# A gated linear recurrence with a low-rank mixer: the first pair's up product taken early and put right later, a bitwise sign, wider filler matmuls and a new order

## The chip, the cores and the metric

The kernel runs on one core of one Trainium2 chip. The metric is the device time of one execution in microseconds. The kernel before took 640.84 us in the median of three runs (638.37 to 641.07).

## The reference

Two blocks stand one behind the other. The first is a recurrence over 768 tokens for 4 batches and 8 heads of 48 channels, with a complex decay for each channel; the second mixes tokens through a rank of 32 and channels through a hidden layer of 1536.

```python
mag = np.sqrt(a_re * a_re + a_im * a_im)
scale = np.minimum(mag, 0.999) / (mag + 1e-06)
ar, ai = a_re * scale, a_im * scale
for t in range(S):                       # S_re, S_im: 48 x 48 per head
    new_re = ar[t] * S_re - ai[t] * S_im
    new_im = ar[t] * S_im + ai[t] * S_re
    S_re, S_im = new_re + k[t] (x) v[t], new_im
    y[t] = q[t] @ S_re
x = y, heads side by side                # 4 x 768 x 384
u = x + (xT @ U @ V)T                    # U: 768 x 32, V: 32 x 768
out = u + np.maximum(u @ w_ch1, 0) @ w_ch2
```

All values are float32.

## The kernel before, in words

**Tiles.** A chunk is 128 tokens of one batch, so there are 24 chunks, six for each batch; a group is two chunks, and a pair of chunks is also the unit of the second block (`mixer(m)`, m from 0 to 11).

**Gates (`gates(g)`).** For a group, the real and imaginary parts of the gates are loaded (`ar`, `ai`), and ACT and DVE turn them into log magnitudes `l` (tile `GL`; from the fourth group on two rounded halves, `GS`) and angles in turns `z` (kept in `y`). The angle takes the sign of `ar`, kept in `n`: in group 0 DVE makes plus or minus one half (`is_ge` and a subtraction, line 656), in the others ACT takes Sign (line 374 is the helper's). Then `z` is the product of `n` and an arctangent less a quarter of pi (line 737), followed by a scale and the addition of 0.25, on DVE in group 0 (line 740) and on ACT as Identity in the others. TensorE forms running sums over tokens by products with triangular matrices: `es ps` and `ef ps` from `l` (line 674), `tot` for block totals (line 712), `ph` from `z` (line 776). ACT's Exp of these gives the factors `es`, `ef` and `E`; Sin of the phase `F` gives `cs`.

**Chunks (`prep(i)`, `chain(i)`).** `prep` multiplies q and k with the factors (`qk`, `QKC`) and transposes them (`tr`, line 834) into `QK`. `chain` forms the products of queries and keys inside blocks (`inner`, lines 884 and 881; `corners`, line 948), scales `QK` between them on DVE, collects the masked blocks in `DG`, moves them by DMA to `AT`, forms the state (`dk`, line 973; `GM`, `G`) and the output `y` (lines 1004 and 1012), which ACT copies into `xo`.

**Mixer.** Once the six chunks of a batch are there, `rank` (line 1047) sums over them with U, ACT copies the result to `r`. For each pair, `spread` multiplies with V (`mixed`, line 1066), DVE adds to `xo`, TensorE transposes (`uTp`), and `uT` feeds the up product: six calls of `up(ff)`, each of two times three matmuls 128x256 (line 1094), whose result ACT copies through Relu to `h`. `down` (lines 1241 and 1284) multiplies `h` with the second weight, DVE adds to `xo`, and a DMA writes it. Pairs from the eighth on take a form with fewer products (`few`, line 1152).

**Order.** Nothing is scheduled when the program runs. Every operation is recorded in `Plan` with its engine and its kind; the table `ORDER` gives each one a place in one list, and `Plan.order()` sorts by it. Every engine executes its own part of that list in order. A second table, `SPARE`, says how many filler matmuls (`idle`, line 1414: the identity with itself, 128x128, into the PSUM tile `spare`) stand ahead of a place. A unit of `SPARE` is one such matmul; a matmul of float32 shows as two records in the profile. In all there are 147 units, 23 of them ahead of the first `es ps`.

**Weights.** The weights come as 64-bit words, 768 KB a piece, and DVE (for later pieces ACT too) converts them (lines 556 to 562); the first pieces are converted in the same stretch as the first chunks.

Of the kernel before, what the change touches and what calls it, by code (L numbers as in the profile page):

```python
# [10 lines left out]
FP = mybir.dt.float32  # L11
# [4 lines left out]
OP = mybir.AluOpType  # L16
# [10 lines left out]

ORDER = {
    ("SP", "load"): {0.1: [5], 1.2: [19], 1: [18], 2: [20], 3.5: [73, 76], 7: [415, 206, 413, 497, 276, 172, 204, 250, 251], 5.1: [99], 5.6: [154],
        6.1: [252], 6.6: [311], 7.1: [492], 7.6: [562], 8.1: [570], 8.6: [620], 9.1: [641], 9.6: [656], 0.0: [2, 1, 2652, 2641, 2654], 0.05: [4, 3],  # L30
        3: [70, 69, 72, 74], 1.3: [71, 68], 1.4: [67], 2.5: [77, 75], 2.6: [209], 5.7: [113, 156], 6: [210], 6.7: [171, 170], 7.7: [312, 279], 8:
        [282], 8.7: [408, 368], 9: [491, 364, 365, 414, 392], 11: [499, 557, 556, 601, 808], 9.7: [604, 488], 10: [560], 10.7: [603, 569], 13: [655,
        643, 682, 644, 976], 11.7: [683, 684], 12: [914], 12.7: [783, 742], 15: [784, 886, 818, 816, 1043], 13.7: [887, 888], 14: [1040], 14.7: [927,
        928], 17: [975, 1041, 1049, 1025, 1307], 15.7: [1057, 1056], 16: [1155], 16.7: [1159, 1154], 19: [1179, 1180, 1237, 1291, 1493], 17.7: [1308,
        1281], 18: [1391], 18.7: [1330, 1366], 21: [1328, 1369, 1454, 1397, 1675], 19.7: [1496, 1453], 20: [1495], 20.7: [1492, 1491], 23: [1591,
        1563, 1578, 1643, 1866], 21.7: [1676, 1677], 22: [1781], 22.7: [1756, 1754], 25: [1837, 1835, 1780, 1867, 2161], 23.7: [1836, 1838], 24:
        [1941], 24.7: [1947, 1943], 25.7: [2162, 2166], 26: [2173], 26.7: [2177, 2167], 27: [2353]},
    ("POOL", "load"): {0: [13], 1.5: [59], 2: [12], 1: [28]},
    ("DVE", "load"): {1: [40]},
    ("DVE", "w1"): {0: [34, 42, 39, 62, 65], 1: [61, 60, 66, 86, 96], 2: [118, 115, 125, 137, 145], 3: [168, 164, 189, 213, 224], 4: [259, 262, 290],  # L40
        5: [355, 379, 429], 6: [348, 381, 559]},
    ("ACT", "w1"): {4: [219, 200], 5: [302, 359], 6: [329, 373]},
    ("ACT", "w2"): {0: [544, 543], 2: [588, 589], 4: [597, 598], 6: [649, 640], 8: [658, 661], 10: [677, 695]},
    ("DVE", "w2"): {0: [565, 566, 568], 2: [593, 594, 605], 4: [606, 621, 624], 6: [651, 653, 654], 8: [659, 670, 671], 10: [699, 700, 703], 12: [704,
        740, 755]},
    ("ACT", "gates"): {0: [0, 7, 6, 11, 16, 21, 23, 36, 53, 43, 44, 45, 55, 58], 1: [14, 8, 22, 29, 30, 37, 46, 54, 48, 49, 52, 57], 2: [127, 104,
        105, 89, 128, 131, 130, 132, 134, 176, 182, 149, 160, 159, 173, 178, 179, 180, 194, 193, 196], 4: [270, 221, 253, 294, 272, 287, 286, 299,
        301, 330, 351, 315, 326, 325, 327, 337, 336, 342, 360, 356, 361], 6: [438, 393, 417, 418, 448, 454, 453, 455, 457, 466, 472, 480, 504, 505,
        503, 508, 509, 510, 496, 495, 511], 8: [582, 584, 602, 583, 610, 612, 613, 618, 619, 623, 627, 628, 660, 650, 657, 664, 665, 667, 639, 638,
        668], 10: [711, 728, 731, 698, 746, 748, 752, 761, 764, 777, 798, 760, 810, 812, 815, 834, 831, 823, 804, 782, 836], 12: [876, 924, 929, 898,  # L50
        932, 944, 950, 952, 951, 986, 997, 973, 981, 982, 985, 1010, 1008, 1011, 993, 994, 1033], 14: [1117, 1106, 1108, 1152, 1135, 1136, 1137, 1173,
        1138, 1174, 1197, 1178, 1196, 1199, 1195, 1212, 1213, 1220, 1208, 1219, 1221], 16: [1273, 1274, 1299, 1272, 1316, 1318, 1317, 1321, 1320,
        1336, 1337, 1322, 1380, 1365, 1363, 1406, 1408, 1402, 1382, 1379, 1413], 18: [1465, 1508, 1506, 1512, 1517, 1518, 1524, 1526, 1529, 1525,
        1537, 1558, 1555, 1557, 1556, 1569, 1567, 1574, 1573, 1568, 1575], 20: [1669, 1665, 1678, 1698, 1697, 1709, 1725, 1734, 1726, 1720, 1735,
        1826, 1771, 1770, 1766, 1800, 1797, 1801, 1774, 1789, 1802], 22: [1889, 1893, 1907, 1890, 1913, 1915, 1914, 1919, 1918, 1933, 1958, 1956,
        1963, 1960, 1957, 1977, 1967, 1969, 1946, 1962, 1978]},
    ("DVE", "gates"): {0: [10, 9, 17, 25, 27, 63, 24], 1: [15, 26, 33, 35, 38, 64, 41], 2: [117, 144, 151, 186], 4: [261, 313, 314, 352], 6: [427,
        465, 473, 475, 483, 535], 8: [607, 622, 632, 633, 634, 642], 10: [736, 753, 765, 766, 776, 799], 12: [931, 945, 961, 966, 969, 1023], 14:
        [1113, 1153, 1185, 1187, 1189, 1236], 16: [1313, 1319, 1339, 1343, 1344, 1358], 18: [1510, 1519, 1544, 1546, 1547, 1559], 20: [1687, 1719,
        1738, 1747, 1748, 1777], 22: [1908, 1926, 1936, 1937, 1939, 1979]},  # L60
    ("PE", "gates"): {0: [31, 32, 51], 1: [47, 50, 56], 2: [158, 161, 174, 175, 192, 191], 4: [323, 324, 335, 340, 343, 341], 6: [502, 501, 506, 507,
        487, 486], 8: [646, 647, 663, 666, 635, 637], 10: [803, 811, 822, 821, 781, 780], 12: [980, 983, 1007, 1006, 992, 991], 14: [1193, 1192, 1211,
        1217, 1204, 1218], 16: [1364, 1356, 1403, 1401, 1381, 1371], 18: [1550, 1549, 1564, 1571, 1572, 1565], 20: [1769, 1764, 1796, 1799, 1773,
        1783], 22: [1959, 1945, 1966, 1968, 1944, 1955]},
    ("SP", "totals"): {0: [98, 79, 80, 97], 2: [198, 208, 195, 211], 4: [410, 409, 411, 391], 6: [498, 558, 500, 561], 8: [741, 681, 685, 680], 10:
        [817, 805, 990, 890], 12: [1157, 1055, 1170, 1042], 14: [1368, 1276, 1367, 1241], 16: [1393, 1392, 1383, 1396], 18: [1755, 1588, 1593, 1594],
        20: [1832, 1942, 1833, 1798], 22: [2176, 2187, 2175, 2174]},
    ("ACT", "angles"): {0: [78, 87, 92, 93, 100], 1: [84, 101, 107, 111, 110], 2: [197, 202, 220, 236, 232, 238, 239, 246, 248, 249], 4: [363, 376,
        390, 406, 396, 397, 398, 421, 430, 431], 6: [545, 564, 587, 615, 626, 673, 674, 708, 707, 710], 8: [669, 675, 709, 750, 773, 841, 842, 813,
        875, 864], 10: [838, 845, 877, 974, 900, 1036, 1037, 1065, 1074, 1071], 12: [1050, 1067, 1081, 1143, 1216, 1267, 1248, 1269, 1245, 1270], 14:  # L70
        [1238, 1246, 1271, 1327, 1346, 1435, 1415, 1462, 1461, 1464], 16: [1414, 1439, 1480, 1531, 1614, 1616, 1615, 1619, 1617, 1668], 18: [1603,
# [1398 lines left out]
```

## Time and profile before

| | |
|---|---|
| median of three runs | 640.84 us (638.37 to 641.07) |
| profiled execution, its span | 641.9 us |
| TensorE busy | 622.8 us (97%) |
| VectorE busy | 509.9 us (79%) |
| ScalarE busy | 396.8 us (62%) |
| spare matmuls | 294 records, 43.9 us busy, from 1.4 to 125.7 us |
| up product of the first pair | from 126.6 us |
| granted clock of TensorE | 0.992 in the mean |

The page gives no time outside the span, so the profiled execution is taken at 641.9 us, 1.1 above the median. "Busy" is the union of an engine's instructions. Matmuls overlap in the array, so a busy TensorE is not one at its full rate, and a record is longer than the distance to the next: where many stand back to back, the distance is what one costs. The window rows show, for each stretch, its length and then, for each engine, the busy time and the count; behind them the clock that TensorE was granted, the busy share of the DMA engines and GB/s. A line in order of time has its start, its length, the engine and line, and in brackets the idle time before it with what ended it.

### The profile page before, as it was taken

What the parts mean: (1) busy time and instruction counts of PE and PEld (TensorE: products, weight loads), DVE (VectorE), ACT (ScalarE), POOL (GpSimd) and SP (SyncE); (2) the same over time, 40 slices, a digit from 0 to 9 for tenths busy, and PEclk for the clock granted to TensorE, in tenths of its full rate; (3) what the DMA queues carried; (4) which work ended last, traced back from release to release, by engine and by line L of the source; (5) the groups of instructions that cost most, each with busy time, mean ns of one, the idle gap of its engine ahead of it and who ended that gap; (6) DMA issues with size and microseconds to landing.
All of it is one profiled execution on the core that took longest, in us unless ns stands there. A gap on an engine that the chain in (4) does not pass through costs nothing.

```text
span 641.9 us, 23713 instructions
## 1 busy us (share of the span) xinstructions
PE 622.8 (97%) x10516; PEld 548.0 (85%) x10516; DVE 509.9 (79%) x923; ACT 396.8 (62%) x765; POOL 38.7 (6%) x79
## 2 busy tenths in 40 slices
PE   8888997999999999999999999999999999999998
PEld 7767776686789988889988989798999998999997
DVE  6998997678999989678877868788999975473743
ACT  7898997788887787876776676687532432102020
POOL 5000000000001010010010100010000000000001
PEclk9999999799999999999999999999999999999999
DMA  7766534745233362333331332611104010000002
GB/s 202 166 148 138 125 70 102 180 119 131 51 66 69 58 126 50 67 69 68 71 77 34 75 74 43 117 37 21 32 20 81 8 42 12 7 1 1 20 1 74
DMA packets 173686, 45.76 MB, mean 71 GB/s; under 512 B 167632, under 2 KB 170384, under 8 KB 173584
## 3 DMA queue, kind: packets, MB, share of 16 engines
q1 hardware_dynamic: 171376, 39.90, 29.4%
q0 software_dynamic: 2208, 4.35, 2.0%
q8 instruction: 82, 1.34, 0.9%
q14 instruction: 20, 0.16, 0.1%
HBM read 33.59 MB, written 4.72 MB: 60 GB/s over the span
## 4 chain that ended last, share of the span: by engine, by line
PE 72%; issue 9%; ACT 7%; DMA 6%; DVE 4%; SPq 3%; POOL 0%; DVEq 0%; ACTq 0%; POOLq 0%
PE down L1284 22%; PE up L1094 11%; PE few L1152 10%; PE y L1012 3%; DMA AT<-DG 3%; PE tr L834 3%; PE dk L973 3%; PE down L1241 3%; ACT gate L374 2%; PE y L1004 2%; PE inner L884 2%; PE inner L881 2%; PE mixed L1066 1%; PE spare L1414 1%; PE tot L718 1%
## 5 line engine op out<-in xcount | busy, mean ns | idle before, releaser
L1094 PE MATMUL up<-uT,w 128*128 128x256 f32 x504 | 116.1, 383 | 0.0
L377 DVE TENSOR_TENSOR QK<-QK,T 112x512 f32<-112x512 f32 (+2 forms) x144 | 101.3, 728 | 7.1 <-PE corners L948 2.6
L1094 PEld LDWEIGHTS up<-uT,w 128*128 128x128 f32 x504 | 93.8, 190 | 12.8
L374 ACT ACTIVATE gate<-gate 128x768 f32<-128x768 f32 (+1 forms) x89 | 70.1, 798 | 8.1 <-DVE GS L768 3.1
L1284 PE MATMUL down<-w,h 128*128 128x192 f32 x396 | 73.5, 331 | 0.0
L845 ACT COPY QK<-tr 112x512 f32<-112x512 f32 x96 | 53.2, 584 | 32.2 <-PE tr L834 31.8
L1284 PEld LDWEIGHTS down<-w,h 128*128 128x128 f32 x396 | 64.1, 190 | 2.7 <-issue 1.5
L1160 ACT COPY h<-few 128x512 f32<-128x512 f32 x30 | 17.3, 586 | 60.9 <-PE few L1152 60.9
L380 DVE TENSOR_TENSOR xo<-down,xo 128x192 f32<-128x192 f32 (+1 forms) x79 | 29.9, 384 | 26.5 <-PE down L1284 26.3
L377 DVE TENSOR_TENSOR QKC<-qk,cs 128x768 f32<-128x768 f32 x48 | 45.4, 952 | 5.2 <-PE tr L834 4.5
L1414 PE MATMUL spare<-ident 128*128 128x128 f32 x294 | 43.9, 295 | 1.4 <-POOL ident masks.py:199 1.4
L1414 PEld LDWEIGHTS spare<-ident 128*128 128x128 f32 x294 | 38.1, 200 | 6.0 <-issue 2.0
L1284 PE MATMUL down<-stage 128*128 128x192 f32 x198 | 37.2, 331 | 0.0
L1152 PE MATMUL few<-gate,w 128*128 128x128 f32 x280 | 35.4, 276 | 0.0
L834 PEld LDWEIGHTS tr<-ident,QKC 64*112 64x112 f32 x768 | 25.9, 130 | 10.7 <-issue 3.3
L834 PE MATMUL tr<-ident,QKC 64*112 64x64 f32 x768 | 33.1, 223 | 1.9 <-ACT QK L845 0.8
L759 POOL DMA_DIRECT2D gate<-F x15 | 11.9, 796 | 379.1 <-DVE F L782 225.3
L1152 PEld LDWEIGHTS few<-gate,w 128*128 128x128 f32 x280 | 33.4, 192 | 0.1
L1284 PEld LDWEIGHTS down<-stage 128*128 128x128 f32 x198 | 32.1, 190 | 1.5 <-DVE stage L1276 0.6
L953 ACT COPY AT<-corners 32x128 f32<-32x128 f32 x96 | 24.2, 255 | 12.1 <-PE corners L948 10.5
L371 ACT ACT_TABLE_LOAD x24 | 30.8, 1283 | 1.1 <-PEq L1454 0.7
L1228 POOL DMA_DIRECT2D out_dram<-xo x32 | 18.5, 606 | 207.2 <-DVE xo L380 119.6
(156 smaller groups left out, 1245.9 us busy)
## 6 DMA issues: line engine op xcount, KB each, us to landing
stage<-in_moe_w_ch_dram SPq DMA_DIRECT2D x12, 768.0 KB, 4.7
gate<-in_a_im_dram SPq DMA_DIRECT2D x24, 192.0 KB, 3.3
gate<-in_a_re_dram SPq DMA_DIRECT2D x24, 192.0 KB, 3.2
VP<-in_v_dram SPq DMA_DIRECT2D x24, 192.0 KB, 3.4
qk<-in_k_dram SPq DMA_DIRECT2D x24, 192.0 KB, 3.3
qk<-in_q_dram SPq DMA_DIRECT2D x24, 192.0 KB, 3.3
AT<-DG SPq DMA_DIRECT2D x96, 32.0 KB, 2.4
T<-E SPq DMA_DIRECT2D x48, 48.0 KB, 2.5
```

The lines of the kernel that those rows point to most:

```text
L371: ACT(1.37, rank, lambda: nc.scalar.preload_act_table_set(name), writes=[TABLE])
L374: return nc.scalar.activation(out=o, in_=i, func=f, **kw)
L377: nc.vector.tensor_tensor(out=o, in0=a, in1=b, op=OP.mult)
L380: nc.vector.tensor_tensor(out=o, in0=a, in1=b, op=OP.add)
L834: nc.tensor.transpose(out=get(*ps[r])[0:DQ, h], in_=get(*qkc)[at, h].rearrange("p u d -> p (u d)")[:, 0:DQ], identity=ident[at, at], tile_ ...
L845: nc.scalar.copy(out=to, in_=a)
L953: ACT(0.36, RR, lambda r=r, u=u: nc.scalar.copy(out=get(*ATi).rearrange("p (a u) t -> p a u t", u=2)[r:r + BLK, :, u, BLK:2 * BLK], in_=ge ...
L973: nc.tensor.matmul(out=get(*dk[r])[x:end, h], lhsT=get(*ks)[at, h, x // DP, 0:end - x], rhs=get(*VPi)[at, h], start=True, stop=True, tile_ ...
L1094: nc.tensor.matmul(out=get(*ps)[:, e], lhsT=w1[:, f, (ff + e) * 128:(ff + e + 1) * 128], rhs=get(*uT)[:, f], start=(f == 0), stop=(f == KD ...
L1152: nc.tensor.matmul(out=get(*ps)[:, q], lhsT=w()[:, q * 128:(q + 1) * 128], rhs=v[0](), start=(n == 0 and q == 0), stop=True, skip_group_ch ...
L1284: nc.tensor.matmul(out=get(*to)[:, part], lhsT=x(j), rhs=y[:, j], start=(first and j == 0), stop=(j == KH - 1), skip_group_check=not first)
L1414: nc.tensor.matmul(out=spare[0], lhsT=ident, rhs=ident, start=True, stop=True)
```

## The change

1. **The first pair's up product.** For m = 0 the turn and `up` now take `xo` before the mixing is added, so they need only the pair's two chunks; ACT copies the result without Relu. Once `r` is there, `put_right` makes up for it. `rT` is r transposed with its two halves added (through the new constant `fold`), `rw ps` its product with the first weight, in four column strips of 32, and ACT copies it to `rw`. `fix` multiplies it with V, two hidden pairs at a time in two PSUM tiles, and DVE adds each to `h` and takes the maximum with zero in one instruction. The two down products of this pair take the hidden pairs in the order of `PUT`.
2. **Bitwise sign.** In groups 0, 1 and 2, `n` is made on DVE: the sign bit of `ar` joined to the bits of 1/pi. The scale of `z` is gone, and the addition of 0.25 becomes a matmul of the triangular matrix with the constant `fourth`, ahead of the one with `z`. The later groups are as before.
3. **Fillers.** Consecutive units of `SPARE` are joined, up to four, into one matmul of the identity with up to 512 columns. There are 117 units: 67 ahead of the first `es ps`, 50 behind it, and the last ahead of the third chunk's `inner`.
4. **Order.** All of `ORDER` is new; the first chunk's gates now stand ahead of the second's. The loads of the first two groups and of the weights stand in another order on SP.

```diff
-SPARE = {31: 23, 47: 2, 51: 1, 83: 11, 94: 3, 106: 7, 114: 4, 122: 5, 146: 8, 158: 1, 212: 9, 215: 3, 263: 8, 266: 4, 281: 6, 303: 2, 307: 5, 323: 1,
...
+SPARE = {26: 67, 75: 4, 97: 3, 103: 4, 115: 4, 125: 4, 127: 2, 128: 4, 147: 5, 168: 4, 207: 5, 231: 1, 258: 3, 269: 4, 289: 3}
...
+    BITS = range(SPLIT[0])
+    PUT = (0, 2), (4, 6), (8, 10)
...
+    nc.vector.tensor_tensor(out=fold, in0=ident[:, 0:R], in1=ident[:, R:2 * R], op=OP.add)
...
-            if on_dve:
-                DVE(c_one(W), R1, lambda: nc.vector.tensor_scalar(out=t(n), in0=t(ar), scalar1=0.0, scalar2=0.5, op0=OP.is_ge,
-                                                                  op1=OP.subtract), AR, [N])
+            if g in BITS:
+                DVE(c_one(W), R1, lambda: nc.vector.tensor_scalar(out=t(n).bitcast(U32), in0=t(ar).bitcast(U32), scalar1=0x80000000,
+                                                                  scalar2=INV_PI, op0=OP.bitwise_and, op1=OP.bitwise_or), AR, [N])
...
-            if on_dve:
-                DVE(c_one(W), R2, lambda: nc.vector.tensor_scalar(out=t(z), in0=t(z), scalar1=2.0 / math.pi, scalar2=0.25, op0=OP.mult,
-                                                                  op1=OP.add), [], Z)
-            else:
+            if g not in BITS:
                 ACT(ca + 0.09, R2, lambda: act(t(z), t(z), AF.Identity, scale=1.0 / math.pi, bias=fourth), [], Z)
...
-                PE(0.65, R2, lambda: nc.tensor.matmul(out=get(*ps), lhsT=prefix, rhs=of(z, i), start=True, stop=not carry),
+                PE(0.65, R2, lambda: nc.tensor.matmul(out=get(*ps), lhsT=prefix, rhs=fourth.to_broadcast([128, DM]), start=True, stop=False),
+                   [("prefix", 0)], [ps], steps=2)
+                PE(0.65, R2, lambda: nc.tensor.matmul(out=get(*ps), lhsT=prefix, rhs=of(z, i), start=False, stop=not carry),
...
-            PE(0.85, R0, products, [r, ("V", 0), uT + ("kept",)], ps, way=5, steps=8)
+            PE(0.85, R0, products, [r, ("V", 0)] + ([uT + ("kept",)] if m else []), ps, way=5, steps=8)
...
-            ACT(c_act(2 * N) - 0.045, R0, lambda: act(get(*h)[:, ff:ff + 2], get(*ps), AF.Relu), [ps], [h + (ff,)])
+            ACT(c_act(2 * N) - 0.045, R0, lambda: act(get(*h)[:, ff:ff + 2], get(*ps), AF.Relu if m else AF.Copy), [ps], [h + (ff,)])
+
+        def put_right():
...
+                    nc.tensor.matmul(out=get(*turned_r)[:, f], lhsT=get(*r)[0:2 * R, f * 128:(f + 1) * 128], rhs=fold[0:2 * R], start=True, stop=True)
...
+                        nc.tensor.matmul(out=get(*weighed)[n * R:(n + 1) * R, 0:k * 256], lhsT=rT()[:, f], rhs=columns,
+                                         start=(f == 0), stop=(f == KD - 1), tile_position=(0, n * R))
...
+                            nc.tensor.matmul(out=get(*ps)[:, e], lhsT=get(*rw)[p, at:at + 128], rhs=V[p, c0 * CH:c0 * CH + N],
+                                             start=True, stop=True, tile_position=(n * R, 0))
+                PE(0.9, R0, products, [rw + (both[0] // 8,), ("V", 0)], pairs, way=7, steps=8)
+                for ps, ff in zip(pairs, both):
+                    o = lambda ff=ff: get(*h)[:, ff:ff + 2]
+                    DVE(c_dve(2 * N), R0, lambda ps=ps, o=o: nc.vector._custom_dve(
+                        dve_ops.TENSOR_ADD_SAT, out=o(), in0=get(*ps), in1=o(), s0=math.inf, s1=0.0), [ps], [h + (ff,)])
...
-                    PE(0.98, RM, lambda half=half: products(half), reads(half) + [("w2s", 0)],
+                    PE(0.98, RM, lambda half=half: products(half), reads(half) + [("w2s", 0)] + ALL_W2,
...
+        if m == 0:
+            for cc in range(MC):
+                turned(cc)
+            for ff in range(0, KF, 2):
+                up(ff)
+            put_right()
...
+            spare.append(pools["psM"].tile([128, 4, 128], FP, tag="psM", name="spare"))
+        nc.tensor.matmul(out=spare[0][:, :k], lhsT=ident, rhs=ident.unsqueeze(1).to_broadcast([128, k, 128]), start=True, stop=True)
```

In the built program, the six `up` of the first pair stand on TensorE between the third chunk's `inner` and the sixth chunk's `y`, and `put_right` behind the low-rank sum. SP issues the same number of loads.

## The prediction

> **What bounds the kernel now.** I read the page's busy shares first, then the busy time by stage, the spare matmuls, the start in order of time, and the chain that ended last.
>
> ```profile
> PE 622.8 (97%) x10516; PEld 548.0 (85%) x10516; DVE 509.9 (79%) x923; ACT 396.8 (62%) x765; POOL 38.7 (6%) x79
> ```
>
> TensorE looks like the bound everywhere. The stages say otherwise (columns: PE, weight loads, DVE, ACT, POOL, then clock and DMA):
>
> ```profile
> 18.00:108.00 90.00, 80.71 (x2012) 64.88 (x2012) 86.03 (x146) 82.39 (x153) 0.00 (x0) 1.00 0.56 127
> 108.00:122.00 14.00, 12.10 (x216) 8.82 (x220) 7.82 (x11) 6.70 (x15) 0.00 (x0) 0.63 0.53 121
> 122.00:166.00 44.00, 43.89 (x308) 32.49 (x304) 34.40 (x50) 38.02 (x60) 2.49 (x3) 1.00 0.48 123
> 166.00:260.00 94.00, 94.00 (x2002) 83.69 (x1996) 88.19 (x151) 74.55 (x146) 5.71 (x9) 1.00 0.37 75
> 260.00:420.00 160.00, 159.92 (x2821) 139.90 (x2813) 123.13 (x216) 113.15 (x221) 9.52 (x15) 1.00 0.35 69
> ```
>
> Up to 108 us VectorE is the bound: 4.0 us idle in 90, while TensorE's share is filled with spares (43.9 us of them, below). Around 108 to 122 the first batch's low-rank sum is waited for, at a clock of 0.63. From 166 us TensorE is full, VectorE nearly so until 260.
>
> ```profile
> L1094 PE MATMUL up<-uT,w 128*128 128x256 f32 x504 | 116.1, 383 | 0.0
> L1164 DVE CUSTOM_DVE_ANT_1 h<-few,h 128x512 f32<-128x512 f32 x30 | 19.9, 685 | 3.7 <-PE few L1152 3.2
> L1414 PE MATMUL spare<-ident 128*128 128x128 f32 x294 | 43.9, 295 | 1.4 <-POOL ident masks.py:199 1.4
> ```
>
> The start, in order of time (start, length):
>
> ```profile
> 1.42 7.18 PE L1414 MATMUL spare<-ident 128*128 128x128 f32 x46 [1.42 <-POOL ident masks.py:199]
> ...
> 8.86 0.54 DVE L380 TENSOR_TENSOR GL<-GL,gate 128x384 f32<-128x384 f32 x1
> ...
> 9.54 0.88 PE L674 MATMUL es ps<-GL,mid 128*128 128x384 f32 x2 [0.94 <-DVE GL L380]
> ...
> 10.26 0.81 PE L674 MATMUL ef ps<-GL,fore 128*128 128x384 f32 x2
> 10.46 0.87 ACT L374 ACTIVATE es<-es ps 128x384 f32<-128x384 f32 x2 [0.24 <-PE es ps L674]
> ...
> 10.91 0.61 PE L1414 MATMUL spare<-ident 128*128 128x128 f32 x4
> ...
> 17.77 0.55 DVE L737 SCALAR_TENSOR_TENSOR gate<-gate 128x384 f32<-128x384 f32 x1
> ```
>
> The spares end before the first `es ps` needs TensorE. Two records of 384 columns take 10.91 - 10.26 = 0.65 us, 0.325 each; that scales to 0.433 for 512 columns.
>
> And the end of the front, in the chain that ended last:
>
> ```profile
> 102.77 7.40 DMA AT<-DG
> ...
> 113.95 1.87 PE dk L973 x26
> ...
> 118.30 1.88 PE y L1012 x32
> ```
>
> Later 32 records of that y line take 1.07 us and 57 of dk 1.07: here the clock was halved. AT's landing is 7.40 us against a median of 2.4 on the page.
>
> **The change, part by part.**
>
> *First spares.* 67 units stand ahead of the first `es ps`, as 16 matmuls of 512 columns and one of 384. Each shows as two records: 32 x 0.433 + 0.65 = 14.5 us at full clock. Before, the 46 records of 128 columns should have taken 46 x 0.108 = 5.0 us by the pitch of 384 columns, and took 7.18 with the tail of the last (0.2), so the slow start costs about 1.9. The block then ends at 1.4 + 14.5 + 1.9 = 17.8 us; without the slow start 15.9. GL of the first chunk is due earlier than before, 8 to 9 us, since ACT and DVE now do that chunk ahead of the second. So `es ps` starts at 17.8 instead of 9.54 and waits on nothing but spares. Behind it on ACT, in order, stand the copies of es and all of the second chunk's Ln and Exp; behind those on DVE the second chunk's sums. ACT reads es 0.92 us after the matmul starts (10.46 - 9.54): 18.7. Fourteen activations (about 0.45 each), a table load (1.28) and Arctan follow: the first z (17.77 before) can start at about 27. By the order of the built program DVE has 12.2 us of work ahead of it (11.3 before, same durations); since DVE starts at 4.48, its idle time grows from 2.0 to about 10.2. The weight conversions it holds are in that 12.2. **+8** (6 to 9).
>
> [...]
>
> *Bitwise sign.* On groups 1 and 2, ACT loses Sign and Identity, four passes of 128x768 at 0.94: -3.7 us. DVE gains two at 0.553 (the 128x768 one-input row, L560) and loses two of group 0 at 0.356: +0.4. In its place six matmuls of 128x384 at 0.65 run while TensorE waits: 3.9 us, covered by time that spares held; without cover 3.9. Summed in order, DVE's work ahead of the sixth chunk's first `rest` operation is 98.7 us against 97.3. **+1.4**, as DVE is the bound.
>
> *The moved up product.* Six ups of 12 records at 2.59 (chain row: 12 records, 2.59 us) and the pair's six uTp records at 0.109, 0.65 together: 16.2 us leave the stage after the low-rank sum and stand between the third chunk's `inner` and the sixth's `y`. Their cover is the time that spares fill now (50 units are left there of 124). Each can hold back a waiting transpose or `y` by up to 2.6; I take +1 in all (0 to 4).
>
> *The correction.* rT, six records of 32 columns: 0.3. `rw`: side by side in column strips as `rank` (24 records in 2.07) 3 x 2 x 0.433 = 2.6; one after another 7.8; I take 2.6, rank being the same form. `fix`: 24 records of 256 columns at 0.216 one by one 5.2, in pairs 2.6; `mixed`, the nearest in form, gains a factor 1.5, so 3.5. TensorE together 6.4 (5.5 to 13.3). DVE: six adds at 0.685 and a copy of at most 0.55: 4.4. ACT: two copies, 0.8, and it lost more. Net on TensorE after the sum: 6.4 - 16.2 = **-9.8**.
>
> *Wait for the sum.* The sixth chunk's `rest` start to the last `rank` took 107.7 to 122.6 = 14.9 us, with the halved clock and the late AT. An up now stands right ahead of y, and loads stand elsewhere: at normal clock the 10 us of slow work take half, at most -5 each for clock and AT, overlapping. **-5** (0 to -7).
>
> *Other waits.* The wait for w2 on `down_two` stands behind sums of the same w2, and `spread` of the first pair only loses one: 0; SP's queue has the same number of loads in another order. The re-plan of all that follows: 0 (-3 to +3), since TensorE is full and its work after the seventh chunk's `inner` is the same within 0.5 us.
>
> **Sum.** The sum is ready at 122.6 + 8 + 1.4 - 5 = 127. TensorE has 9.8 us less to do then; DVE has not. From the sixth chunk's `rest` to the seventh's levels DVE holds 43.8 us of work (40.4 before, in 56.1 us, 15.7 of them idle). It starts at 107.7 + 9.4 = 117.1. Idle between 0 and 10.7 (15.7 less the 5): 160.9 to 171.6; I take 6, since w2 conversions fill some of it: 166.9 against 163.8, **+3.1**. With +1 for the ups in the way: **+4**. TensorE's saving goes into waiting for DVE, and from there the same work follows. The profiled execution spans 641.9 us, 1.1 above the median of 640.84 (the page gives no time around the span); 640.84 + 4 = **645**.
>
> **Rivals.**
> 1. *Slower, the above* (0.50): the block of spares delays a front that DVE bounds. For it: 4.0 us idle in 90. About a fifth of it still lies within 0.5%.
> 2. *Faster: TensorE stays the bound* (0.25). DVE's idle time of 15.7 us takes up the stall, so only TensorE counts after the sum: +4.4 - 9.8 = -5.4, 635.5. For it: 166 to 625 us is TensorE's. Against: DVE's 43.8 us from 117.1 leave only 2.9 us of idle before it is late. It decides at 3 us of idle there. It holds too if the first GL is late, its loads being behind w1's: then the block costs nothing; but the first chunk's two are still the first two loads, and both had landed by 4.48.
> 3. *No change* (0.13): idle about 3, ups not in the way: 641.
> 4. *The front goes cold* (0.07): with 50 spares where 124 were, waits halve the clock as at 111 to 121; that doubled dk and y. Two such stretches at 4 us on top of 645: 653. [...]
> 5. *The ups do not move in time* (0.05): their w1 pieces are converted late behind the stall and they run after the sum: +4.4 + 6.4 = +11, 652.
>
> **How the numbers follow.** 0.5%, 3.2 us, is what a measurement of this kernel can tell. Faster: nearly all of rival 2, 0.23. Same: rival 3, a fifth of 1 and the rest of 2, 0.25. Slower: 0.52. Rival 1's ends are -2.9 - 3 and +7.8 + 3 around the median: 635 to 652; reaching to the far side of 2 and to 4 and 5: 634 to 654.
>
> **What would show it.** Right: `es ps` first at 17 to 18 us with spares before it; DVE idle there some 7 us and 86 of 90 busy after; `rank` at about 126; no halved clock at 111; TensorE with gaps between 127 and 167 on DVE's account. Wrong: first `es ps` near 9, or `rank` before 123, or the seventh chunk's levels before 161; then rival 2.

## The result: slower by 1.5%, and the profile after

The changed kernel took 650.64 us in the median of four runs (646.28 to 652.9); runs of the kernel before beside it took 639.61 us (638.12 to 641.07). The ratio used here is 1.0149, with an interval of 1.0114 to 1.0184, so the change costs 9.6 us (0.0149 x 641). The quotient of the two medians would be 1.0172, or 11.0 us; for the kernels below, too, the quotient of the medians lies up to 0.004 from the ratio given, so a difference of that size decides nothing. The forecast was 645, in a range of 634 to 654, with "slower" the likeliest case. The profiled execution took 652.9 us, 651.1 of them in its span. That is 1.8 us around the span, so the profile of the kernel before, with a span of 641.9, belongs to an execution of some 643.7 us: about 3 us above the median, where the section on the profile before has 1.1.

The busy shares say as little as before:

```profile
PE 627.6 (96%) x10354; PEld 529.2 (81%) x10354; DVE 515.6 (79%) x931; ACT 396.8 (61%) x763; POOL 39.1 (6%) x79
```

Every engine does nearly the work it did. The start, in order of time, shows the first loss:

```profile
1.43 16.40 PE L1475 MATMUL spare<-ident 128*128 128x512 f32 x34 [1.43 <-POOL ident masks.py:199]
...
17.66 0.81 PE L680 MATMUL es ps<-GL,mid 128*128 128x384 f32 x2
...
18.50 0.49 ACT L378 ACTIVATE es<-es ps 128x384 f32<-128x384 f32 x1 [8.59 <-PE es ps L680]
...
19.99 0.56 DVE L384 TENSOR_TENSOR gate<-gate 128x384 f32<-128x384 f32 x1 [8.32 <-ACT gate L378]
...
21.76 1.34 PE L680 MATMUL es ps<-GL,mid 128*128 128x384 f32 x2 [2.65 <-DVE GL L384]
...
28.14 0.56 DVE L743 SCALAR_TENSOR_TENSOR gate<-gate 128x384 f32<-128x384 f32 x1 [1.49 <-ACT gate L378]
```

Read the brackets down the page. The block of spares ends, `es ps` starts without any wait of its own, ACT had been idle 8.59 us for it, and VectorE 8.32 us for ACT. The first angle (line 743) starts at 28.14 instead of 17.77: 10.4 us late. Part of that comes from the `es ps` of the second chunk at 21.76: it takes 1.34 us for what the first one does in 0.81, as the clock was halved from 22.1 us on.

The windows show the clock as well (length, then busy time and count of PE, weight loads, DVE, ACT and POOL, then the granted clock, the DMA share and GB/s):

```profile
18.00:28.00 10.00, 7.00 (x44) 3.53 (x42) 6.35 (x14) 7.66 (x16) 0.00 (x0) 0.83 0.54 116
28.00:108.00 80.00, 71.57 (x1564) 48.57 (x1564) 75.51 (x124) 69.35 (x130) 0.00 (x0) 0.96 0.56 129
108.00:135.00 27.00, 23.77 (x568) 19.91 (x572) 19.75 (x35) 21.56 (x44) 0.00 (x0) 0.87 0.51 116
135.00:166.00 31.00, 27.85 (x142) 15.19 (x137) 27.25 (x40) 26.15 (x40) 1.22 (x2) 0.89 0.51 133
166.00:180.00 14.00, 13.95 (x217) 10.09 (x216) 13.58 (x22) 11.84 (x20) 2.27 (x3) 1.00 0.45 92
180.00:260.00 80.00, 79.47 (x1644) 70.52 (x1643) 74.51 (x126) 66.23 (x129) 4.63 (x7) 1.00 0.36 70
```

The column before the last two is what matters. It was 1.00 in 18 to 108 us and 0.63 in 108 to 122 before; now it is under 1 in each stretch up to 166 us. By the clock's own record, the changed kernel runs at half clock at 22.1 to 25.5, 97.1 to 104.0, 110.8 to 117.6 and 138.1 to 144.9 us, 23.9 us together; the kernel before did so at 111.0 to 121.2 alone. From 166 to 650.1 us the clock is whole, and TensorE is busy for 480.9 of these 484.1 us.

In the chain that ended last, two of the early ups take 5.0 and 4.5 us for 12 records where one takes 2.6 to 2.8 at whole clock:

```profile
99.56 4.98 PE up L1104 x12
...
109.69 3.11 issue
...
114.18 4.51 PE up L1104 x12
```

The sum's first product `rank` starts at 133.8 us (115.8 before), and the first `down` at 148.4 (144.1). From there the lag stays between 8 and 12 us to the end.

### The profile page after: what moved, and what is told of

The parts are those of the page before. It is cut to its first block, busy times and chain, and to the rows that moved or that the text cites. A ratio compares the mean times of both kernels' runs of the same rounds, so it can differ in the third digit from the quotient of the medians.

```text
span 651.1 us, 23423 instructions
## 1 busy us (share of the span) xinstructions
PE 627.6 (96%) x10354; PEld 529.2 (81%) x10354; DVE 515.6 (79%) x931; ACT 396.8 (61%) x763; POOL 39.1 (6%) x79
## 3 DMA queue, kind: packets, MB, share of 16 engines
q0 software_dynamic: 2208, 4.35, 1.9%
## 4 chain that ended last, share of the span: by engine, by line
PE 83%; DVE 7%; ACT 6%; issue 2%; DMA 1%; SPq 0%; POOL 0%; DVEq 0%; ACTq 0%; POOLq 0%
PE down L1337 23%; PE up L1104 17%; PE few L1203 10%; PE tr L839 4%; PE y L1017 3%; PE dk L978 3%; PE spare L1475 3%; PE inner L889 2%; PE y L1009 2%; PE mixed L1071 2%; PE inner L886 2%; PE tot L724 2%; ACT gate L378 1%; PE down L1294 1%; DVE QK L381 1%
## 5 line engine op out<-in xcount | busy, mean ns | idle before, releaser
L1104 PE MATMUL up<-uT,w 128*128 128x256 f32 x504 | 120.8, 393 | 0.0
L1104 PEld LDWEIGHTS up<-uT,w 128*128 128x128 f32 x504 | 96.3, 195 | 14.1
L762 POOL DMA_DIRECT2D gate<-F x15 | 12.4, 827 | 376.5 <-DVE F L787 219.0
L378 ACT ACTIVATE h<-up 128x512 f32<-128x512 f32 x42 | 24.7, 597 | 12.7 <-PE up L1104 12.6
L1475 PE MATMUL spare<-ident 128*128 128x512 f32 (+3 forms) x66 | 30.5, 590 | 1.4 <-POOL ident masks.py:199 1.4
L958 ACT COPY AT<-corners 32x128 f32<-32x128 f32 x96 | 24.4, 256 | 11.7 <-PE corners L953 10.2
```

Source lines behind the costliest of these rows:

```text
L378: return nc.scalar.activation(out=o, in_=i, func=f, **kw)
L958: ACT(0.36, RR, lambda r=r, u=u: nc.scalar.copy(out=get(*ATi).rearrange("p (a u) t -> p a u t", u=2)[r:r + BLK, :, u, BLK:2 * BLK], in_=ge ...
L1104: nc.tensor.matmul(out=get(*ps)[:, e], lhsT=w1[:, f, (ff + e) * 128:(ff + e + 1) * 128], rhs=get(*uT)[:, f], start=(f == 0), stop=(f == KD ...
L1475: nc.tensor.matmul(out=spare[0][:, :k], lhsT=ident, rhs=ident.unsqueeze(1).to_broadcast([128, k, 128]), start=True, stop=True)
```

## The experiments

All ratios are against runs of the kernel before on the same chip, whose median moved between 639.6 and 644.7 us from one series of runs to another; so versions are compared by ratio, and 0.001 is 0.64 us. The clock and the places in time are those of the profiled run. For the short block alone that run took 647.47 us, 3.8 above the kernel's median, so its row shows the kernel later than it mostly is. Runs of the kernel before itself show how time and clock go together: 44 runs at 0.996 or more have a median of 642.3 us, 23 runs between 0.991 and 0.9955 one of 645.0, and 16 runs under 0.9905 one of 646.4.

| kernel | ratio to before | interval | clock | first `es ps`, first `rank` |
|---|---|---|---|---|
| changed | 1.0149 | 1.0114 to 1.0184 | 0.981 | 17.7, 133.8 |
| short block | 0.9975 | 0.9930 to 1.0020 | 0.979 | 8.6, 126.3 |
| before, long block | 1.0036 | 0.9995 to 1.0077 | 0.997 | 17.0, 117.6 |
| short block, 26 late fillers | 1.0064 | 1.0029 to 1.0100 | 0.989 | 8.9, 127.9 |
| short block, late ups | 1.0231 | 1.0161 to 1.0301 | 0.956 | 8.6, 125.7 |
| before, fewer fillers | 1.0095 | 1.0059 to 1.0130 | 0.958 | 10.0, 121.0 |
| short block, 64 fillers | 1.0007 | 0.9974 to 1.0041 | 0.992 | 8.5, 125.8 |
| short block, no correction | 0.9999 | 0.9972 to 1.0026 | 0.981 | 8.6, 123.2 |
| short block, fillers in gaps | 0.9953 | 0.9925 to 0.9981 | 0.995 | 8.5, 120.8 |
| the same, last up behind the sum | 0.9974 | 0.9941 to 1.0007 | 0.997 | 8.9, 121.7 |
| long block, 64 fillers | 1.0106 | 1.0066 to 1.0147 | 0.997 | 18.6, 133.2 |
| fillers in gaps, late ups | 1.0258 | 1.0229 to 1.0287 | 0.984 | 8.6, 125.3 |
| long block, fillers in gaps | 1.0065 | 1.0029 to 1.0102 | 0.995 | 17.8, 128.5 |

### 1. The first block alone

```diff
-SPARE = {26: 67, 75: 4, 97: 3,
+SPARE = {26: 22, 75: 4, 97: 3,
...
```

> The changed kernel with 22 spare units ahead of the first es product where it has 67; nothing else differs. Theory 1 (the block of spares holds back a front that VectorE bounds, and nothing later gives it back): the first es product starts at about 8.5 us where it started at 17.66, the first angle at 18 to 20 where it was 28.1, and the time falls by 8 to 10 from 650.6, to about 641.5. Rival (the wait is taken up by idle time of VectorE after 108 us, and the loss lies in the halved clock or in the new order): the start moves in the same way, the time stays at 647 or more.

It took 643.64 us (637.04 to 648.28), at 0.9975: no longer distinguishable from the kernel before, and the interval lies wholly under the changed kernel's. The step is 0.0174, or 11.2 us, so the loss hangs for the most part on the 45 units taken out here. `es ps` starts at 8.6 us as in the kernel before, `rank` at 126.3.

The counterpart, the kernel before with the long block:

```diff
-SPARE = {31: 23, 47: 2, 51: 1,
+SPARE = {31: 60, 47: 2, 51: 1,
...
```

> The kernel before with 60 spare units ahead of its first es product where it has 23: the 37 more take 37 x 0.223 = 8.3 us at the pitch of its own spares. Nothing else differs. Theory 1: the first es product starts at about 17.8 where it started at 9.54, the low-rank sum is late by about 8, and the time rises by 7 to 9 from 639.6, to about 648. Rival (the wait is taken up later): 640 to 642.

Here the block costs little: 1.0036, about 2.3 us, with an interval that touches 1; theory 1 missed, and the rival held. `es ps` is 7.4 us late and the first angle 6.2, yet `rank` only 1.9. The windows of this kernel show where the delay went:

```profile
18.00:108.00 90.00, 83.20 (x1922) 66.90 (x1920) 82.98 (x138) 82.86 (x155) 0.00 (x0) 0.98 0.51 114
108.00:122.00 14.00, 13.66 (x373) 10.67 (x376) 12.74 (x21) 11.78 (x27) 0.00 (x0) 1.00 0.75 160
```

VectorE is busy 12.74 of the 14 us around the sum, where it was 7.82 before. The late work runs in VectorE's idle time there, and the clock stays whole in it. In this kernel the wait for the sum could take in most of a late front.

### 2. Fillers and the clock

The changed kernel has 50 units behind the first block where the kernel before has 124. To see what fillers do by themselves, 52 were taken out of the kernel before, all those between 63 and 126 us:

```diff
-... 281: 6, 303: 2, 307: 5, 323: 1, 349: 2, 371: 7, ... 577: 2, 581: 1}
+... 281: 6}
```

> The kernel before, with the 52 units of spare products that lie after place 281 left out (95 of 147 units stay, among them the 23 of the first block); nothing else changes. Theory 1 (what the changed kernel lost beside its longer first block, it lost because fewer spare products stand in TensorE's idle time, and the granted clock is halved more often): the mean clock falls from 0.997 to about 0.987, as in the changed kernel with the short block (0.987), halved stretches of 6.8 us turn up between 60 and 125 us, and the time rises by 4 to 5 us, which is what the runs of the kernel before lose between a clock of 0.997 (641 to 642.5) and one of 0.987 (645.6 to 647.5). Theory 2 (the spare products only fill time, and the clock does not hang on them here): the clock stays at 0.997, and the time is the same or some tenths of a us lower, as up to 52 x 0.28 = 14 us of TensorE's work is gone from a part where VectorE sets the end.

It took 650.32 us: 1.0095, or 6.1 us, a little more than expected, and the clock fell much further. Two windows of the kernel before:

```profile
56.00:108.00 52.00, 46.39 (x1277) 37.85 (x1277) 48.23 (x82) 48.02 (x89) 0.00 (x0) 1.00 0.46 100
108.00:136.00 28.00, 26.05 (x290) 20.14 (x291) 17.57 (x27) 17.52 (x31) 0.96 (x1) 0.82 0.54 134
```

and the same two without the 52 fillers:

```profile
56.00:108.00 52.00, 39.16 (x1072) 31.23 (x1075) 43.51 (x72) 43.41 (x80) 0.00 (x0) 0.75 0.38 79
108.00:136.00 28.00, 26.71 (x368) 19.85 (x359) 17.45 (x31) 17.71 (x33) 0.51 (x1) 0.50 0.67 160
```

The clock of 1.00 becomes 0.75, and then 0.50 for the whole of 28 us. VectorE's share falls too, 43.5 us busy for 48.2 in the first window. Its waits that are put down to TensorE stay as they were there (3.5 us for 3.6); 4.9 us put down to ScalarE are new, all but 0.2 for its work on TensorE's results (`xo` and `F`), so the way from the slower TensorE to VectorE is argued, not shown. That fewer fillers halve the clock and cost time, which is rival 4's mechanism, is shown with nothing else changed.

Can fillers be put back into the changed kernel? Three tries behind the short block. (The numbers of added units in the expectations are miscounted; the text has the right ones: 26, 64 and, for the late ups, 45.) In these kernels a filler behind place 289 takes a PSUM buffer of its own anew. The first put 26 units at eight late places:

```diff
-SPARE = {26: 67, 75: 4, ... 269: 4, 289: 3}
+SPARE = {26: 22, 75: 4, ... 269: 4, 289: 3, 431: 6, 436: 3, 461: 3, 479: 2, 497: 2, 523: 2, 596: 5, 626: 3}
```

> The kernel with 22 spare units at the start, and 27 units more between the fifth chunk's first transposes and the correction, where the changed kernel's TensorE had waits and its clock was halved (97, 111 and 138 us). Theory 1 with the second part (three stretches of halved clock cost 5 to 8 us on the way to the low-rank sum and just behind it): the clock stays whole from 28 to 150 us, an up of 12 records takes 2.6 to 2.9 everywhere, and the time is 4 to 6 below the kernel with 22 units alone, about 637. Rival (the slow clock fell into time in which TensorE waited anyway): the time is that of the kernel with 22 units alone within 1.5.

A miss: 646.13 us, 1.0064, slower than without them. At one place a filler even made TensorE wait, for its PSUM buffer, which an up product held until ACT had copied it:

```profile
113.24 0.70 PE L1483 MATMUL spare<-ident 128*128 128x256 f32 x2 [1.73 <-ACT h L386]
```

The second try added 64 units, at the front's places too:

```diff
+SPARE = {26: 22, 50: 8, 56: 2, 75: 10, 97: 4, 103: 8, 115: 6, 125: 5, 127: 2, 128: 6, 147: 7, 168: 4, 207: 6, 231: 1, 258: 6, 269: 6, 289: 4, 431: 8, 436: 4, 461: 4, 472: 6, 479: 4, 497: 3}
```

> The changed kernel with its first block cut to 22 units, and 51 more units of spare products put where its trace shows TensorE idle: 8 ahead of the second half's fore and mid products (idle 3.4 us there), 6 more ahead of the first angles, 1 to 4 more at seven places up to the third pair's levels, and 29 between the third and fifth chunks (idle 1.9 us ahead of the transposes, 3.3 us after the levels). Theory 1: with as many spare products as the kernel before (124 units in all) the clock stays whole as often as there (0.997), and the time comes to 637 to 638, which is what the runs of the short block give at a clock of 0.992 to 0.997 (637.0 to 642.4 measured at 0.992); this would be the fastest kernel yet. Theory 2 (the clock follows something else, or the added products stand in the way of work that waits): clock 0.984 to 0.992 and 643 to 647, as with the 27 added units tried before (646.1).

The clock came back (0.995 in the mean of ten runs, as in the kernel before) but the time did not: 645.47 us, 1.0007. Half of theory 1 held. The likely reason is that the added products took what the clock gave, where TensorE had no pause to put them in. The third try, with 58 units added, left out 16 of the late ones, 15 of them because TensorE had no pause behind them, and put 10 where the trace still showed it waiting:

```diff
+SPARE = {26: 22, 50: 12, 56: 2, 75: 10, 97: 4, 103: 8, 115: 6, 125: 5, 127: 2, 128: 6, 147: 7, 168: 4, 207: 6, 231: 1, 258: 6, 269: 6, 289: 4, 431: 7, 472: 6, 596: 4, 626: 2}
```

> The changed kernel with the short first block (22 units) and added spare products only where the trace with the 51 added units still shows TensorE waiting for data: 12 ahead of the second half's products (1.7 us were still idle behind 8), the front's as there, 7 ahead of the fifth chunk's transposes, 6 ahead of its levels, 4 ahead of the transposition of r (idle 1.3 us) and 2 ahead of the fix products (0.8 us). The 15 units between the third and fifth chunks after which TensorE was not idle are left out (15 x 0.29 = 4.4 us of TensorE's work). Theory 1 (added products cost time exactly where TensorE does not wait, and hold the clock wherever they stand): clock 0.990 to 0.995 and 640 to 642, under the short block alone (643) and under the kernel before. Theory 2 (the time that the added products took is not that of the places, but of the whole kernel): 644 to 646, as with 51 units.

641.25 us against 644.7 for the kernel before beside it: 0.9953 (0.9925 to 0.9981). This is the fastest version, and faster than both kernels. Its interval just overlaps that of the second try (from 0.9974), so that the places matter is likely and not shown. Against the short block alone (0.9975) the intervals overlap too, so how much of it is the fillers' is not settled behind a short block. Behind the long one it is, next.

### 3. The block and the fillers, each at whole clock

```diff
-SPARE = {26: 22, 50: 8, ...          (64 fillers)
+SPARE = {26: 67, 50: 8, ...
```

> The changed kernel with its own long first block (67 units) and all 51 added spare products of the earlier run at whole clock. Theory 1 (the long block costs by the later start of the gates, whatever the clock): clock about 0.995, and 6 us more than the same kernel with the short block (645.5): 651 to 652. Theory 2 (the long block cost time by the state of the clock that followed it): 645 to 647 at the same clock.

651.43 us, as theory 1 said, at a clock of 0.995 in the mean: 1.0106 against 1.0007 with the short block, 6.3 us. So the block's price does not come through the clock.

```diff
-SPARE = {26: 22, 50: 12, ...         (fillers in gaps)
+SPARE = {26: 67, 50: 12, ...
```

> The changed kernel with its own long first block (67 units), and the spare products in the idle places that went with 641.25 us behind the short block. Against that kernel it prices the block alone, at whole clock on both sides; against the changed kernel it prices the fillers alone. Theory 1 (the block costs some 6 us by the later gates, fewer fillers cost some 4 us by the clock, and the two add up): 647 to 648, clock 0.995. Theory 2 (behind the long block the clock costs nothing that fillers could give back): 650 to 652.

648.73 us and 1.0065 (1.0029 to 1.0102), a hit for theory 1 within about a microsecond. This kernel lies between two others that differ from it in one thing each. Short block to long block: 0.9953 to 1.0065, 7.2 us. Then fewer fillers, which is the changed kernel: 1.0065 to 1.0149, 5.4 us. None of these three intervals overlaps another. The split depends on the order of the steps, though: with the fillers taken out first, behind the short block, they cost 1.4 us (0.9953 to 0.9975, not clear of nothing) and the block then 11.2 (0.9975 to 1.0149). So, by the order of the steps, the block costs 6 to 11 us and the fewer fillers 1 to 5; the two together cost 12.6. Its windows show the front at whole clock:

```profile
18.00:28.00 10.00, 9.93 (x57) 5.32 (x56) 7.27 (x16) 8.07 (x17) 0.00 (x0) 1.00 0.53 114
28.00:108.00 80.00, 75.47 (x1643) 50.76 (x1642) 75.69 (x125) 71.57 (x133) 0.00 (x0) 1.00 0.57 132
108.00:131.00 23.00, 22.20 (x519) 17.89 (x519) 20.39 (x35) 20.49 (x41) 0.00 (x0) 1.00 0.61 144
```

The first angle starts at 27.08 us here (28.14 in the changed kernel) and `rank` at 128.5 (133.8).

How a delay travels is seen best in a table. For each VectorE operation that both kernels have, I took its start less its start in the profile of the kernel before; the median of each stretch, in us:

| stretch (time before) | changed | before, long block | long block, fillers in gaps | short block, fillers in gaps |
|---|---|---|---|---|
| 30 to 45 | 10.2 | 6.2 | 9.6 | 1.6 |
| 90 to 105 | 14.6 | 6.2 | 11.0 | 3.8 |
| 120 to 135 | 13.8 | 0.3 | 7.5 | -0.1 |
| 135 to 150 | 8.9 | 0.2 | 2.7 | -6.1 |
| 165 to 180 | 8.9 | 0.6 | 3.9 | -4.2 |
| 270 to 285 | 10.8 | 0.6 | 5.0 | -2.3 |
| 630 to the end | 9.0 | 0.1 | 6.1 | -3.3 |

The last two columns differ by 8.0 in the first row, 7.2 to 8.8 in those between, and 9.4 at the end: the block's delay is carried through whole. In the kernel before it was gone by 120 us. Part of that column's zeros is the profile of before itself, which had 10.2 us of halved clock just there; its ratio (2.3 us) is the better measure.

### 4. The early up products

```diff
-    ("PE", "mixing"): {0: [303, 438, 328, 486, 561, 505, ...
+    ("PE", "mixing"): {0: [604.1, 604.2, 607.6, 612.6, 615.6, 619.6, ...
...
```

> The kernel with 22 spare units at the start, and the six up products of the first pair, their copies and the start of the correction placed behind the mixing product of the first pair, where the kernel before has them; all the same instructions. The ups then use nothing of the front. If TensorE is the bound behind the low-rank sum (rival 2 of the prediction): 15.5 us more of TensorE work there, less what the front no longer holds back: +10 to +15 over the kernel with 22 units alone, about 653. If VectorE bounds the stage from the sum to the seventh chunk (the prediction's step that let TensorE's saving vanish): +0 to +5.

659.77 us, 1.0231; but with the ups gone from the front nothing filled it, and the clock was 0.53 from 90 to 130 us, so this mixes two things. The same edit with fillers in the ups' old places:

```diff
+SPARE = {26: 22, 50: 12, ... 289: 4, 301: 5, 345: 2, 380: 6, 431: 7, 436: 4, 465: 3, 472: 6, 497: 6, 551: 2, 604: 4}
```

> The changed kernel with the short first block and spare products in the idle places (the one that took 641.25 us), but the first pair's six up products, their copies and the transposition of r stand behind the mixing product again, as in the kernel with late ups tried before; 43 spare products (12 us) fill their old places, so that the clock stays whole. This prices the early up products at equal clock. Theory 1 (the early ups lay half in idle time: three of them, 8.6 us, stand on the path to the sum, so the sum comes earlier when they go, and the stage after it is 15.5 us longer): rank at 115 to 118 us, clock 0.99 or more, 641.25 + 15.5 - 4 = 652 to 653 (650 to 655). Theory 2 (VectorE sets the sum whatever TensorE does ahead of it): rank at 120 to 121, 641.25 + 15.5 = 656 to 658. If it were under 645, the early ups would be worth next to nothing and the gain over the kernel before would be the fillers' alone.

661.36 us, 1.0258: slower than either theory said. `rank` came at 125.3, no earlier than with the ups ahead of it (120.8). But the clock was not held: ahead of `rank` it was halved for 20.5 us (69.2 to 76.0, 96.5 to 103.3 and 113.6 to 120.4), for 3.4 us with the early ups (91.4 to 94.8). So this run does not tell whether the early ups delay the sum; it prices the stage behind the sum, where the clock was whole in both. In order of time, the stage behind the mixing product with late ups:

```profile
129.12 0.92 PE L1079 MATMUL mixed<-r,V 64*128 64x192 f32 x8
129.97 5.45 PE L1112 MATMUL up<-uT,w 128*128 128x256 f32 x24
...
135.61 10.52 PE L1112 MATMUL up<-uT,w 128*128 128x256 f32 x48
146.06 0.85 PE L1125 MATMUL rT<-fold,r 64*128 64x32 f32 x6
```

and with early ones (fillers in gaps):

```profile
124.92 1.42 PE L1079 MATMUL mixed<-r,V 64*128 64x192 f32 x8
126.76 0.62 PE L784 MATMUL ph<-GS,prefix_r 128*128 128x384 f32 x2 [0.41 <-DVE xo L392]
127.31 2.77 PE L1134 MATMUL rw ps<-w,rw 128*32 128x512 f32 x24
...
130.84 1.16 PE L1150 MATMUL fix<-V,rw 32*128 32x256 f32 x16
...
133.33 0.91 PE L1302 MATMUL down<-w,h 128*128 128x384 f32 x2 [0.16 <-DVE h L1155]
```

From `mixed` to the first `down` it is 23.6 us with late ups and 8.4 with early ones: the move takes 15.2 us out of this stage, at equal clock in it.

Do the ups cost time where they now stand? One was moved behind the rank products:

```diff
-    ("PE", "mixing"): {0: [303, 438, 328, 486, 561, 505, ...
+    ("PE", "mixing"): {0: [303, 438, 328, 486, 590, 505, ...
...
```

> As the kernel with spare products in the idle places alone, but the last of the six early up products (the fifth pair of blocks) is issued after the sum's rank products, where TensorE waits 1.3 us for r, instead of 3 us ahead of them; the four spare products there are left out. Theory 1 (ups between 104 and 125 us stand on TensorE's path to the sum, which runs without a pause there): the rank products start 2.9 us earlier, 1.3 us of the up lie in the wait for r, the rest goes back: 1.3 us less than the kernel with all six ahead, so 639 to 641. Theory 2 (VectorE's rest of the sixth chunk sets the sum, and the up lies beside it): rank starts no earlier, and the time grows by the 1.6 us that do not lie in the wait for r.

643.19 us, 0.9974, with a `rank` at 121.7 (120.8 with all six ahead): theory 2's mechanism for this one up. TensorE, freed of 2.9 us of work there, waited 1.53 us and started this `y` no earlier (119.94 for 119.12):

```profile
119.94 0.79 PE L1017 MATMUL y<-VP,AT 64*64 64x48 f32 x32 [1.53 <-DMA AT<-DG]
```

The sum hangs on the blocks that come through the DMA into `AT`, and the up lies beside that wait. The difference to 0.9953 is within the intervals.

### 5. The correction

```diff
-            put_right()
...
```

> The changed kernel with its first block cut to 22 units and the rank-32 correction left out: no transposition of r, no product of it with w1, no fix products and none of the six additions into h (the first pair's hidden values then lack the mixing part). By the prediction's sum this takes 6.4 us of TensorE and 4.4 us of VectorE out of the path after the sum: theory 1 expects 643.6 - 6.4 = 637 (636 to 639). Theory 2 (the stage after the sum waits for the second layer's weights or for VectorE's other work, and the correction lies beside it): 642 to 644.

644.23 us, 0.9999: without the correction nothing is gained against the short block's 0.9975 (the intervals overlap). TensorE, in order of time:

```profile
128.94 1.01 PE L776 MATMUL ph<-GS,prefix_r 128*128 128x384 f32 x2 [1.37 <-DVE xo L384]
134.31 1.19 PE L776 MATMUL ph<-GS,prefix_r 128*128 128x384 f32 x2 [4.35 <-DVE GS L770]
135.29 4.92 PE L1294 MATMUL down<-w,h 128*128 128x384 f32 x10
```

TensorE stands idle 4.35 us for VectorE, and the clock is halved from 128.1 to 138.4. With the correction its products lie in that gap, so its time on TensorE is hidden here. What it would cost at whole clock was not tried.

## Why the prediction was right, and where it was not

**The sign and the mechanism held.** The block of spares delays a front that VectorE bounds, and the delay reaches the end: rival 1. Its price is 7.2 us with the fillers in gaps (6.3 with 64 fillers, 11.2 with the changed kernel's own), where the delay of the front was put at +8 (6 to 9). From the fastest version, three steps lead to the result: -3.0 (that version against before), +7.2 (the block), +5.4 (fewer fillers) = +9.6. They add up by construction, since each is the difference of two ratios in a row. The forecast of +4 lacks 5.6. That the time still lies in the range is owed to its wide ends (rival 1 alone reaches to 652, for idle time and for the re-plan), and not to a term for what made the difference.

**Where the 5.6 us are.** The sum goes in three parts, and each can be read from the traces: from the first angle (17.77 us before) to the sixth chunk's `rest` on VectorE, from there to the end of the last `rank`, and from the same `rest` to the seventh chunk's levels. All in us; the last two columns are VectorE's in the first part:

| kernel | first angle | sixth `rest` | to the last `rank` | to the levels | VectorE busy | VectorE idle |
|---|---|---|---|---|---|---|
| before | 17.8 | 107.7 | 15.0 | 56.2 | 85.9 | 4.0 |
| predicted | 27 | 117.1 | 9.9 | 49.8 | 87.3 | about 4 |
| changed | 28.1 | 125.3 | 10.7 | 48.6 | 87.8 | 9.4 |
| long block, fillers in gaps | 27.1 | 119.5 | 11.2 | 49.3 | 87.4 | 5.0 |
| short block, fillers in gaps | 18.9 | 112.8 | 10.2 | 48.0 | 87.6 | 6.4 |

**First spares, +8.** The block was to end at 17.8; `es ps` started at 17.66. The first angle was to start at 27; it did at 27.08 with the clock held, and at 28.14 in the changed kernel, whose clock halved at 22.1 us. So +8 was right but for the clock.

**The step that missed: the front's clock, put at nothing.** The sum lets the front run to the sixth chunk's `rest` at 107.7 + 9.4 = 117.1, with VectorE "86 of 90 busy" as before. It came at 125.3, 8.2 late. From the first angle on, VectorE's work was as predicted (87.8 us, 1.8 more than before, where the part on the sign has 1.4), but it was idle for 9.4 us instead of 4.0, while the clock of TensorE was halved at 97.1 to 104.0 and 110.8 to 117.6. With the fillers put back into gaps, and the clock whole up to 134.9 us, the same `rest` comes at 119.5 and `rank` at 128.5 instead of 133.8; VectorE is idle for 5.0 us. So 5.8 of the 8.2 us go with the fillers and the clock. The other 2.4 are there at whole clock too, and no run says which part of the new order makes them. Held clock alone is not enough: with 64 fillers it was whole from 78.7 us on, and `rank` still came at 133.2.

**Wait for the sum, -5.** This held. From the sixth `rest` to the last `rank` it was 10.7 us for the 9.9 predicted. The halved clock of 111 to 121 us did not go away, as the prediction had it; it lay ahead of this stretch in the changed kernel.

**Rival 4, the front goes cold, 0.07.** This is what happened, on top of rival 1: 5.4 us by the step above, where the rival has 8. The chance was far too small. The prediction knew that 50 units stand where 124 had been, and used the spares' time as cover for the ups, but priced what the spares were holding up only in a rival. Listing it beside the block was also wrong, as the two do not exclude each other: it belonged into the sum.

**The moved up product.** 16.2 us were to leave the stage; 15.2 did. Whether +1 for ups in the way was right is open: moving one of them away brought the sum no earlier, and the run that moved all six had another clock. That two of them took 5.0 and 4.5 us goes with the halved clock (97.1 to 104.0 and 110.8 to 117.6).

**The correction.** TensorE 6.4 us predicted; `rT` 0.85, `rw ps` 2.77, `fix` about 2.3 (16 records in 1.16 and 8 in as much) are 5.9. The six adds were predicted at 0.685 and took 0.684. Leaving all of it out did not show in the time, at a halved clock.

**TensorE's saving goes into waiting for VectorE.** Right, and well sized: from the sixth `rest` to the seventh levels the changed kernel took 48.6 us for the 49.8 predicted: VectorE was busy for 42.2 (43.8 predicted) and idle for 6.3 (6 taken). In the fastest version the stage after the sum is 12.4 us shorter than in the kernel before (8.4 against 20.8 from `mixed` to the first `down`), and 3 us of it reach the end; the last column of the table shows it going, -6.1, -4.2, -2.3. The seventh chunk's levels, predicted 3.1 us late, came 10.0 late (173.8), since the sixth `rest` was already 8.2 later than predicted.

**Bitwise sign, other waits, the re-plan.** No run tells these apart; in the front they are among the 2.4 us above. From 180 to 420 us the changed kernel's lag stays between 8.5 and 11.5 us, so behind the first pair the re-plan costs at most some 2 us. The bitwise operations take 0.354 and 0.555 us, as was assumed. VectorE's busy time in the front grew by 1.5 to 1.8 us, near the predicted 1.4; what the sign costs by itself was not tried.

## What to carry to other kernels

Before counting filler work as free time for something else, ask what it does for the clock: take some out and read the granted clock by window (52 units fewer in the kernel before: 0.75 for 1.00 in 56 to 108 us). Put fillers where the trace shows the engine waiting, not merely where it is thinly used: here the version with fillers in gaps was the fastest, while 26 late and 64 spread ones gained nothing. A delay at the start of a stage costs its full length only if no idle time of the bounding engine lies ahead (a first angle 6.2 us late cost about 2.3 us in the kernel before; one 8.2 us late cost 7.2 in the new order, with the fillers in gaps), so count that idle time in the changed kernel, not in the old one.

## What the runs showed of the hardware

**When the clock halves.** In all fourteen traces the clock changes only on a grid of 3.413 us (in the changed kernel from 22.1 to 97.1 us it is 22 steps, to 110.8 another 4, to 138.1 another 8). Sorting the windows of this grid from about 10 to 160 us by TensorE's busy share in them: of 29 windows at full clock with less than 0.60, 24 were followed by a halved one; of 33 between 0.60 and 0.75, 6; of 136 between 0.75 and 0.95, 4; of 328 above that, none. In the traces of the kernel before and the changed one alone it was 3 of 4, 2 of 7, none of 21 and none of 44. The way back is stricter: of 21 halved windows with a share under 0.95, none was followed by full clock, and of 55 above it, 35 were (none of 2, and 5 of 8, in these two traces). A busy share counts records, whose ends are modelled, so the bounds are rough.

Before none of the drops up to 160 us in these two traces did TensorE pause for a whole step of the grid: the longest pause was 3.11 us, at 109.69 us. The drop at 97.1 us follows a window in which TensorE was busy for 0.26 of the time and its longest pause was 2.51 us; those at 110.8 and 138.1 us follow shares of 0.60 and 0.62. In the kernel before, the window ahead of the drop at 111.0 us was busy for 0.32 with no pause over 1.40 us.

**Half clock in a busy stretch.** With late ups, the short block's kernel sat at half clock for 37 us on end (91.1 to 128.6) while TensorE counted as busy for 33 of the 40 us from 90 to 130. A halved product counts as busy for longer (`es ps` took 1.34 us for 0.81), so the busy row alone does not show that the work slows; the clock column does.

**Open.** One pause of 3.1 us inside the fifth chunk's `inner` products at 109.69 us is named "issue", so nothing the profile shows ended it; it is 2.2 us in the kernel with 64 fillers. What it waits for was not found.
